# A gated MLP computed in rows, w_out's last rows on 16, 15 and 9 lanes, and an output of 360 and 280 columns with one store

## The chip, the cores and the metric

The kernel runs on one core of a Trainium2 chip. The metric is the device time of one execution in microseconds; for before it is the median of three runs. The engines are TensorE (PE, matmuls and transposes), VectorE (DVE), ScalarE (ACT), GpSimd (POOL) and SyncE (SP), which here only issues loads. 16 DMA engines move the data of all queues.

## The reference

One token of four sequences goes through a layer norm, then attention over a cache of 4096 positions in 32 heads of 128, and beside it a gated MLP; both are added to the token.

```python
xn = _layernorm(x, axis=-1)                       # x: 4 x 1 x 640, bf16
# attention
q = (xn @ wq).reshape(B, 1, 32, 128)              # wq: 640 x 4096
scores = einsum('bhqd,bhkd->bhqk', q, k_cache) * 128 ** -0.5   # caches: 4 x 32 x 4096 x 128
o = einsum('bhqk,bhkd->bhqd', softmax(scores), v_cache)
a = o.reshape(B, 1, 4096) @ wo                    # wo: 4096 x 640
# gated MLP
z = gelu(xn @ w_in)                               # w_in: 640 x 1728, tanh form
z1, z2 = z[..., :864], layernorm(z[..., 864:])
g = w_sp * z2 + b_sp                              # 1 x 1 and 1
m = (z1 * g) @ w_out                              # w_out: 864 x 640
out = x + a + m
```

The two caches are 268 MB of the 282 MB that are read.

## The kernel before

**Units.** The attention runs in 16 units: a unit is one batch and one group of 8 heads. Its keys and its values are 8.39 MB each. Each head takes 16 lanes, each lane 256 positions of 128 numbers, cut into four quarters (`NK = 4`).

**Places.** Keys go to `k_ring`, a ring of 7 quarters. Values go to `v_all`, which holds one unit. At the start `v_all` holds the weights: wq in its first 20,480 columns, w_in behind it, then the five full rows a lane of w_out. The rest of w_out lies in `p_m`, the place of the softmax's weights later on: one more row on 128 lanes, and 8 rows on each of 12 lanes, which are loaded in four loads of three lanes (`W_OUT`, `load_part`).

**The steps of a quarter n** (loop at L739): `product` (L537) multiplies the keys by the query on VectorE, `fold_half` (L543) adds halves on VectorE, `sums` (L555) adds the rest up on TensorE, and after every second quarter `row_sums` (L569) reads the result. At the end of a unit come the maximum, the exponentials (ScalarE), `by_head` (L607) and, a quarter later, `weighted` (L631), which multiplies by the values.

**The order of the loads** is a list (L195 to L203) that `pump` goes through: a load is written into the program as soon as the place it needs is marked free by the steps before it in the program. All of them are issued by SP, in this order, and each waits there for the semaphores of whatever it overwrites. There are eight semaphores for loads, given out in turn, so that a load also waits for an earlier one that used the same semaphore. The first entries are two quarters of unit 0's keys, `load_w` (w_in and the first parts of w_out), the other two quarters of unit 0, `load_w_few` (the part on few lanes), and unit 1's keys. `pump` runs for the first time at L237, ahead of the code for q. Unit 1's keys overwrite the quarter that unit 0's first step has used, so they wait for the first `sums`. Unit 0's values overwrite the weights in `v_all`, so they wait for the gated MLP. Unit 2's keys wait for the first `sums` of unit 1.

**q** (L297 to L314): 40 matmuls, chunk by chunk of wq (five rows a lane, 4096 columns each), into two PSUM tiles, which VectorE scales into `q_rows`. `stage_q` (L515) spreads the query of one unit over the lanes.

**The gated MLP** (`gmlp`, L397) is a generator whose pieces the loop calls in steps 0 and 1: z is made in columns (features on lanes), 140 small matmuls; gelu, the norm and the gate follow on VectorE and ScalarE; the products with w_out are 28 matmuls (L503) into `out_ps`, which x has entered already (L373).

**The output.** `out_ps` holds the 640 columns as two groups of 320, on lanes 0 to 3 and 32 to 35. At the end one copy (L823) takes both to SBUF, and two stores, on ScalarE's and SP's queues, write them.

Of the kernel before, what the change touches and what calls it, by code (L numbers as in the profile page):

```python
# [17 lines left out]
def kernel(  # L18
# [43 lines left out]
    W_OUT = ((P, 5, 1), (P, 1, 1), (12, 8, 4))  # L62
    assert sum(n * r for n, r, _ in W_OUT) == Fh
    NFC = sum(r for _, r, _ in W_OUT)

    def up(n):
        return -(-n // 256) * 256

    PW = sum(up(r * D) for _, r, _ in W_OUT[1:])
    NOH = D // 2  # L70
# [30 lines left out]
    nc.scalar.dma_start(out=x_bf, in_=A_x.flatten_outer_dims())  # L101
    v_all = places.tile([P, NK * QW], BF16, name="v_all")
# [6 lines left out]
    w_parts, f0, at_p = [], 0, 0  # L109
    for n, r, t in W_OUT:  # L110
        if f0 == 0:
            room = v_all[0:n, at_v : at_v + r * D]
        else:
            room = p_buf[0:n, at_p : at_p + r * D]
            at_p += up(r * D)
        w_parts.append((room.rearrange("p (k n) -> p k n", k=r), f0, n, r, t))
        f0 += n * r
    nc.sync.dma_start(out=wq_sb, in_=A_wq.rearrange("(p c) n -> p c n", c=DC))

    def load_part(part):  # L120
        w, f0, n, r, t = part
        rows = B_w_out[f0 : f0 + n * r].rearrange("(p k) n -> p k n", k=r)
        for l in range(t):
            nc.sync.dma_start(out=w[l:n:t], in_=rows[l:n:t])
# [12 lines left out]
    w_rows = [  # L137
        (w[:, i], f0 + i, n, r) for w, f0, n, r, _ in w_parts for i in range(r)
    ]
# [83 lines left out]
    def load_wo(hg):  # L223
        rows = A_wo[hg * HT * Dh : (hg + 1) * HT * Dh]
        if hg == HG - 1:
            by_head = rows.rearrange("(h p) n -> p h n", p=P)
            for h0, h1 in ((0, 2), (2, 4), (4, 6), (6, 7)):
                nc.sync.dma_start(out=wo_sb[:, h0:h1, :], in_=by_head[:, h0:h1, :])
            for half in range(2):
                cols = slice(half * NOH, (half + 1) * NOH)  # L230
                nc.sync.dma_start(out=wo_sb[:, HT - 1, cols], in_=by_head[:, HT - 1, cols])
            return
# [50 lines left out]
    wsp_bf = const.tile([1, 1], BF16)  # L283
    bsp_bf = const.tile([1, 1], BF16)
# [81 lines left out]
    out_ps = ps_out.tile([P, NOH], FP32)  # L366
    OG = 32

    def out_sum(half):
        return out_ps[OG * half : OG * half + Bsz, :]  # L370

    for half in range(2):
        nc.tensor.matmul(  # L373
            out=out_ps[OG * half : OG * half + OG, :],
            lhsT=ident[:Bsz, :OG],
            rhs=x_bf[:, half * NOH : (half + 1) * NOH],
            start=True,
            stop=False,
        )

    gm = {}
    for name in ("zz", "gw", "gt"):
        gm[name] = work.tile([P, 2, NFC, Bsz], FP32, name=name)
    gm["gz"] = work.tile([P, 3, NFC, Bsz], FP32, name="gz")
    nc.gpsimd.memset(gm["zz"][:], 0.0)
    gm["st"] = work.tile([1, 5 * Bsz], FP32, name="st")
    gm["ac"] = work.tile([1, 2 * Bsz], FP32, name="ac")
    gm["yT"] = work.tile([P, NFC, Bsz], BF16, name="yT")

    by_lanes = []  # L390
    for n, r, _ in W_OUT:
        if by_lanes and by_lanes[-1][0] == n:
            by_lanes[-1] = (n, by_lanes[-1][1] + r)
        else:
            by_lanes.append((n, r))

    def gmlp():  # L397
        zz, gw, gt, gz = (gm[n] for n in ("zz", "gw", "gt", "gz"))
        zT = ps_pv.tile([P, 2, NFC, Bsz], FP32, tag="pv", name="zT")
        for t in range(2):  # L400
            w_t = w_in_sb[:, :, t * Fh : (t + 1) * Fh]
            for k, (_, f, n, r) in enumerate(w_rows):
                for c in range(DC):
                    nc.tensor.matmul(
                        out=zT[0:n, t, k, :],
                        lhsT=w_t[:, c, f : f + (n - 1) * r + 1 : r],
                        rhs=xnT[:, c, 0:Bsz],
                        start=(c == 0),
                        stop=(c == DC - 1),
                    )  # L410
        yield
        k0 = 0
        for n, ks in by_lanes:
            nc.vector.tensor_copy(
                out=zz[0:n, :, k0 : k0 + ks, :], in_=zT[0:n, :, k0 : k0 + ks, :]
            )
            k0 += ks
        nc.vector.tensor_tensor(out=gw[:], in0=zz[:], in1=zz[:], op=ALU.mult)
        nc.vector.tensor_scalar(
            out=gw[:], in0=gw[:], scalar1=0.044715, scalar2=1.0, op0=ALU.mult, op1=ALU.add  # L420
        )
        nc.vector.tensor_tensor(out=gw[:], in0=gw[:], in1=zz[:], op=ALU.mult)
        nc.scalar.activation(
            out=gt[:], in_=gw[:], func=ACT.Tanh, scale=math.sqrt(2.0 / math.pi)
        )
        yield
        nc.vector.tensor_scalar(
            out=gt[:], in0=gt[:], scalar1=1.0, scalar2=0.5, op0=ALU.add, op1=ALU.mult
        )
        nc.vector.tensor_tensor(out=gz[:, 0:2], in0=zz[:], in1=gt[:], op=ALU.mult)  # L430
        sq = gz[:, 2, :, :]
        nc.vector.tensor_tensor(out=sq, in0=gz[:, 1, :, :], in1=gz[:, 1, :, :], op=ALU.mult)

        s_ps = ps_m.tile([1, 2, NFC, Bsz], FP32, tag="m", name="ln_ps")
        nc.tensor.matmul(
            out=s_ps[:], lhsT=ones_sq[:, 0:1], rhs=gz[:, 1:3], start=True, stop=True
        )
        yield
        st, ac = gm["st"], gm["ac"]
        mean_t = st[:, 0:Bsz]  # L440
        ex2_t = st[:, Bsz : 2 * Bsz]
        var_t = st[:, 2 * Bsz : 3 * Bsz]
        rst_t = st[:, 3 * Bsz : 4 * Bsz]
        tmp_t = st[:, 4 * Bsz : 5 * Bsz]
        nc.vector.tensor_reduce(
            out=st[:, 0 : 2 * Bsz].rearrange("o (s b) -> o s b", s=2),
            in_=s_ps[:].rearrange("o s k b -> o s b k"),
            axis=AX.X,
            op=ALU.add,
        )  # L450
        nc.vector.tensor_scalar(
            out=st[:, 0 : 2 * Bsz],
            in0=st[:, 0 : 2 * Bsz],
            scalar1=1.0 / float(Fh),
            scalar2=None,
            op0=ALU.mult,
        )
        nc.vector.tensor_tensor(out=tmp_t, in0=mean_t, in1=mean_t, op=ALU.mult)
        nc.vector.tensor_tensor(out=var_t, in0=ex2_t, in1=tmp_t, op=ALU.subtract)
        nc.scalar.activation(  # L460
            out=rst_t, in_=var_t, func=ACT.Sqrt, bias=eps_tile[:1], scale=1.0
        )
        wsp_t = work.tile([1, 1], FP32, name="wsp_t")
        nc.gpsimd.tensor_copy(out=wsp_t[:], in_=wsp_bf[:])
        bsp_t = work.tile([1, 1], FP32, name="bsp_t")
        nc.gpsimd.tensor_copy(out=bsp_t[:], in_=bsp_bf[:])
        yield
        nc.vector.reciprocal(out=rst_t, in_=rst_t)
        nc.vector.tensor_scalar(
            out=ac[:, 0:Bsz], in0=rst_t, scalar1=wsp_t[:, 0:1], scalar2=None, op0=ALU.mult  # L470
        )
        nc.vector.tensor_tensor(out=tmp_t, in0=ac[:, 0:Bsz], in1=mean_t, op=ALU.mult)
        nc.vector.tensor_scalar(
            out=ac[:, Bsz : 2 * Bsz],
            in0=tmp_t,
            scalar1=-1.0,
            scalar2=bsp_t[:, 0:1],
            op0=ALU.mult,
            op1=ALU.add,
        )  # L480
        ac_ps = ps_m.tile([P, 2 * Bsz], FP32, tag="m", name="ac_ps")
        nc.tensor.matmul(
            out=ac_ps[:], lhsT=ones_sq[0:1, :], rhs=ac[:], start=True, stop=True
        )
        ac_sb = work.tile([P, 2 * Bsz], FP32, name="ac_sb")
        nc.scalar.copy(out=ac_sb[:], in_=ac_ps[:])
        yield
        nc.vector.tensor_tensor(
            out=sq,
            in0=gz[:, 1, :, :],  # L490
            in1=ac_sb[:, None, 0:Bsz].to_broadcast([P, NFC, Bsz]),
            op=ALU.mult,
        )
        nc.vector.tensor_tensor(
            out=sq,
            in0=sq,
            in1=ac_sb[:, None, Bsz : 2 * Bsz].to_broadcast([P, NFC, Bsz]),
            op=ALU.add,
        )
        nc.vector.tensor_tensor(out=gm["yT"][:], in0=gz[:, 0, :, :], in1=sq, op=ALU.mult)  # L500
        for k, (w, _, n, _) in enumerate(w_rows):
            for half in range(2):
                nc.tensor.matmul(  # L503
                    out=out_sum(half),
# [351 lines left out]
```

## Time and profile before

| what | value |
|---|---|
| median of three runs (lowest, highest) | 662.18 us (661.91, 662.43) |
| the profiled execution | 662.09 us |
| its span, first to last instruction | 660.2 us |
| busy share: VectorE, TensorE, ScalarE, GpSimd | 79%, 48%, 5%, 2% |
| read from memory | 282.24 MB, 428 GB/s over the span |
| mean granted TensorE clock | 0.692 |
| wait of VectorE's `product` for keys | 87.9 us in 13 waits |

The page divides the span into 40 slices and prints for each engine the busy tenths (9 is 90% or more); for the DMA engines it is the mean share of the 16. In the timeline a line is: start us, length us, engine, source line, operation, tile written from tile read, count, and in brackets how long the engine had been idle and what it had waited for. `SPq` is SP's queue of issues. In the list of waits a line is: who waited, for whom, us in total, times, longest.

### The profile page before, as it was taken

To read this page: it belongs to the slowest core of one execution; us is meant where nothing else is said; L and a number is where in the kernel's file an instruction comes from. 1 tells how busy PE (TensorE), PEld (TensorE's weight loads), DVE (VectorE), ACT (ScalarE), POOL (GpSimd) and SP (SyncE) were. 2 spreads that over 40 slices of the span, in tenths; PEclk is the share of its full clock that TensorE was granted. 3 is DMA by queue.
4 is the path that set the end of the run, shared out by engine and by line. 5 is a ranking of instruction groups with operands and counts; after the bars stand their busy time and mean duration, and the time that the engine had idled before them with its cause. 6 is when DMAs were issued, how large, how long until landed. Compare 5 with 4: busy or idle time off the path is not lost.

```text
span 660.2 us, 4777 instructions
## 1 busy us (share of the span) xinstructions
PE 317.0 (48%) x2083; PEld 136.3 (21%) x2083; DVE 522.6 (79%) x276; ACT 29.9 (5%) x73; POOL 10.1 (2%) x20
## 2 busy tenths in 40 slices
PE   0574372526427363452636336263452534737367
PEld 0231121212213121120212112121120211212124
DVE  1767978959597795969959598695969969999950
ACT  0020000000000000000000000000000000000000
POOL 2300000000000000000000000000000000000000
PEclk9757676766767676585767768676685867676785
DMA  9999999999999999999999999999999999999997
GB/s 369 433 461 434 417 441 434 433 437 438 421 445 426 437 430 441 437 422 433 434 441 441 418 437 441 430 441 421 434 441 437 426 421 445 422 427 436 449 409 284
DMA packets 8232, 282.55 MB, mean 428 GB/s; under 512 B 892, under 2 KB 2184, under 8 KB 2568
## 3 DMA queue, kind: packets, MB, share of 16 engines
q1 hardware_dynamic: 8192, 282.25, 99.1%
q8 instruction: 16, 0.26, 0.1%
q10 hardware_dynamic: 20, 0.01, 0.0%
q14 instruction: 4, 0.03, 0.0%
HBM read 282.24 MB, written 0.01 MB: 428 GB/s over the span
## 4 chain that ended last, share of the span: by engine, by line
DMA 62%; DVE 28%; PE 8%; issue 1%; ACT 0%; DVEq 0%
DMA k_ring<-in_A_k_cache_dram 53%; DVE k_ring L537 14%; DVE k_ring L543 7%; PE s_ps L555 6%; DMA v_all<-in_A_v_cache_dram 4%; DMA k_ring<-in_A_wo_dram 3%; DVE s_sb L569 3%; DMA v_all<-in_A_wq_dram 2%; DVE p_m L607 1%; DVE m L578 1%; PE q_ps L303 1%; PE pv L631 1%; PE out_ps L699 1%; DVE p_m L678 1%; DVE mf L580 1%
## 5 line engine op out<-in xcount | busy, mean ns | idle before, releaser
L537 DVE TENSOR_TENSOR k_ring<-k_ring,qbc 128x8192 bf16<-128x8192 bf16 x64 | 282.9, 4420 | 88.5 <-DMA k_ring<-in_A_k_cache_dram 87.9
L555 PE MATMUL s_ps<-k_ring,ident 128*128 128x512 bf16 x512 | 202.2, 566 | 313.8 <-DVE k_ring L543 313.7
L555 PEld LDWEIGHTS <-ident 128*128 128x128 bf16 x512 | 64.0, 130 | 430.0 <-issue 245.4
L543 DVE TENSOR_TENSOR k_ring<-k_ring 128x4096 bf16<-128x4096 bf16 x64 | 145.9, 2280 | 1.1
L631 PE MATMUL pv<-v_all,p_m 128*32 128x512 bf16 x960 | 62.5, 419 | 0.0
L569 DVE TENSOR_REDUCE s_sb<-s_ps 128x128 f32<-128x1024 f32 x32 | 39.0, 1218 | 3.7 <-PE s_ps L555 3.7
L607 DVE TENSOR_TENSOR p_m<-p_c,own 128x2048 bf16<-128x2048 bf16 x16 | 36.6, 2285 | 0.7 <-ACT p_c L596 0.7
L631 PEld LDWEIGHTS <-p_m 128*32 128x32 bf16 x992 | 26.6, 106 | 42.5 <-issue 23.3
L596 ACT ACTIVATE p_c<-s_sb,nm 128x256 bf16<-128x256 f32 x16 | 8.1, 508 | 342.9 <-DVE nm L588 342.9
L662 PEld LDWEIGHTS o_ps<-o_rows,pick 128*128 128x128 f32 x96 | 20.4, 294 | 4.3 <-issue 3.3
L662 PE MATMUL o_ps<-o_rows,pick 128*128 128x128 f32 x96 | 19.1, 367 | 0.0
L643 ACT COPY o_rows<-pv 128x512 f32<-128x512 f32 x16 | 9.4, 586 | 165.7 <-PE pv L631 165.7
L311 DVE TENSOR_SCALAR q_rows<-q_ps 128x512 bf16<-128x512 f32 x2 | 1.4, 692 | 12.8 <-PE q_ps L303 12.8
L817 DVE TENSOR_TENSOR o_n_last<-o_last,rden_all 128x32 bf16<-128x32 f32 x1 | 0.2, 192 | 12.2 <-PE o_last L809 12.2
L303 PE MATMUL q_ps<-v_all,xnT 128*32 128x512 bf16 x40 | 4.5, 630 | 9.3 <-DMA v_all<-in_A_wq_dram 9.3
L527 ACT CAST qbc<-qbc_ps 128x128 bf16<-128x128 f32 x16 | 4.3, 266 | 97.6 <-PE qbc_ps L519 97.6
L578 DVE TENSOR_REDUCE m<-s_sb 128x1 f32<-128x256 f32 x16 | 6.7, 420 | 0.5
L519 PE MATMUL qbc_ps<-q_rows,of_row 128*128 128x128 bf16 x32 | 6.0, 276 | 0.6 <-DVE q_rows L311 0.6
L519 PEld LDWEIGHTS <-of_row 128*128 128x128 bf16 x32 | 4.1, 132 | 8.1 <-issue 7.4
L716 PE MATMUL o_last<-hot,o_rows 128*128 128x8 f32 x32 | 4.9, 279 | 0.7 <-ACT o_rows L643 0.7
L716 PEld LDWEIGHTS o_last<-hot,o_rows 128*128 128x128 f32 x32 | 4.8, 226 | 1.8 <-ACT o_rows L643 1.6
L699 PE MATMUL out_ps<-k_ring,p_m 128*4 128x320 bf16 x48 | 4.0, 309 | 2.1 <-DVE p_m L691 2.1
(87 smaller groups left out, 81.4 us busy)
## 6 DMA issues: line engine op xcount, KB each, us to landing
k_ring<-in_A_k_cache_dram SPq DMA_DIRECT2D x5, 4096.0 KB, 27.2
v_all<-in_A_v_cache_dram SPq DMA_DIRECT2D x2, 4096.0 KB, 28.2
v_all<-in_A_wq_dram SPq DMA_DIRECT2D x1, 5120.0 KB, 15.4
k_ring<-in_A_k_cache_dram SPq DMA_DIRECT2D x2, 2048.0 KB
k_ring<-in_A_v_cache_dram SPq DMA_DIRECT2D x1, 4096.0 KB
k_ring<-in_A_wo_dram SPq DMA_DIRECT2D x3, 1280.0 KB, 20.6
v_all<-in_B_w_in_dram SPq DMA_DIRECT2D x1, 2160.0 KB
k_ring<-in_A_v_cache_dram SPq DMA_DIRECT2D x1, 2048.0 KB
```

The source lines that it names most:

```text
L303: nc.tensor.matmul(out=q_ps[k * QD : (k + 1) * QD], lhsT=xnT[:, c, :], rhs=wq_v[:, c, k, e], start=(c == 0), stop=(c == DC - 1),)
L519: nc.tensor.matmul(out=qb_ps[:], lhsT=of_row[:, e, b].rearrange("p k f l -> p (k f l)"), rhs=q_rows[e][:, hg, :], start=(e == 0), stop=(e ...
L537: nc.vector.tensor_tensor(out=t, in0=t, in1=qbcs[u][:, None, :].to_broadcast([P, HC, Dh]), op=ALU.mult)
L543: nc.vector.tensor_tensor(out=t[:, :, 0:HD2], in0=t[:, :, 0:HD2], in1=t[:, :, HD2:Dh], op=ALU.add)
L555: nc.tensor.matmul(out=s, lhsT=ident[:], rhs=t[:, :, g * RW : (g + 1) * RW], start=(g == 0), stop=(g == m - 1),)
L569: nc.vector.tensor_reduce(out=scores[u][:].rearrange("p (r c) -> p r c", r=NK)[:, lo : hi + 1 : hi - lo], in_=sums_ps.pop(n // 2)[:], axis ...
L578: nc.vector.tensor_reduce(out=m1[:], in_=scores[u][:], axis=AX.X, op=ALU.max)
L607: nc.vector.tensor_tensor(out=p_m[:, u % 2], in0=p_c.pop(u)[:].rearrange("p (g c) -> p g c", c=CB)[:, :, :, None].to_broadcast([P, NG, CB, HT]
L631: nc.tensor.matmul(out=pvs[u][cg * QD : (cg + 1) * QD, :], lhsT=p_m[:, u % 2, g0 + n].rearrange("p c h -> p (c h)"), rhs=v_at[:, n * CB : ...
L662: nc.tensor.matmul(out=gr[hg][:], lhsT=pick[:, c, Bsz - 1 - b : P + Bsz - 1 - b], rhs=o[:, c, :], start=(b == 0 and c == 0), stop=(b == Bs ...
L699: nc.tensor.matmul(out=out_sum(half), lhsT=o, rhs=wo_sb[:, n, half * NOH : (half + 1) * NOH], start=False, stop=(hg == HG - 1 and n == HT ...
L716: nc.tensor.matmul(out=o_last[0][:, :, :, u % Bsz], lhsT=o[:, c, :], rhs=hot[:, c, :].rearrange("p (k e) -> p k e", e=PAR), start=(c == 0) ...
```

## The change

- `W_OUT` becomes four parts: five rows on 128 lanes in `v_all` as before, two rows on 16 lanes in `p_m`, and two parts of eight rows, on 15 and on 9 lanes, at the beginning of `v_all`. The last two use three of every four lanes and are loaded in three loads each; the 15 lanes belong to `load_w`, the 9 to `load_w_few`.
- The 1-element loads of w_sp and b_sp move from behind `stage_q(0)` to the beginning.
- `gmlp` makes z in rows: the four batches stay on lanes, the features lie along the row; four slices of 160 features share the array's column groups, the last 224 follow by themselves. Gelu, the norm and the gate work on rows of 384 numbers for each half. A transpose turns the gated rows into the columns that the products with w_out need, of which there are now 46.
- The scratch `gw` and the transposed `yT` lie in `v_all`, behind the two new parts.
- `out_ps` is cut at 360 columns, in all of x, w_out and wo; the end has two copies (VectorE and ScalarE) and one store.

```diff
-    W_OUT = ((P, 5, 1), (P, 1, 1), (12, 8, 4))
+    W_OUT = (
+        (P, 5, "v", 4, "first"),
+        (16, 2, "p", 4, "first"),
+        (15, 8, "q", 3, "first"),
+        (9, 8, "q", 3, "then"),
+    )
+    CUT = (0, 360, D)
+    places_w = {
+        "v": (v_all, up(DC * (HD + F))),
+        "p": (p_buf, 0),
+        "q": (v_all, 0),
+    }
+    for n, r, home, used, cuts in W_OUT:
+        t, at = places_w[home]
+        places_w[home] = (t, at + up(r * D))
+        lanes = n // used * GAP if used < GAP else n
+        room = t[0:lanes, at : at + r * D].rearrange("p (k n) -> p k n", k=r)
+        w_parts.append((room, f0, n, r, used, cuts))
+        f0 += n * r
+    at_g = places_w["q"][1]
+    def load_part(part, when):
+        w, f0, n, r, used, at = part
+        if at != when:
+            return
+        rows = B_w_out[f0 : f0 + n * r]
+        if used == GAP:
+            nc.sync.dma_start(out=w, in_=rows.rearrange("(p k) n -> p k n", k=r))
         else:
...
+            by_used = rows.rearrange("(q l k) n -> l q k n", l=used, k=r)
+            for l in range(used):
+                nc.sync.dma_start(out=w[l::GAP], in_=by_used[l])
     def load_w():
         nc.sync.dma_start(out=w_in_sb, in_=B_w_in.rearrange("(p c) n -> p c n", c=DC))
         for part in w_parts:
-            if part[4] == 1:
-                load_part(part)
+            load_part(part, "first")
     def load_w_few():
         for part in w_parts:
-            if part[4] > 1:
-                load_part(part)
+            load_part(part, "then")
...
+    zz = work.tile([P, 2, FW], FP32, name="zz")
+    gw = v_all[:, at_g : at_g + 4 * FW].bitcast(FP32).rearrange("p (t f) -> p t f", t=2)
+    at_g += up(4 * FW)
+    yT = v_all[:, at_g : at_g + NFC * QD].rearrange("p (k b) -> p k b", b=QD)
...
+        for c in range(DC):
+            for g in range(NQ):
+                nc.tensor.matmul(
+                    out=z_w[g * QD : (g + 1) * QD],
+                    lhsT=xnT[:, c, :],
+                    rhs=w_v[:, c, :, g * FN : (g + 1) * FN],
...
+        nc.scalar.mul(out=zz[:, :, 0:FN], in_=z_w[:], mul=0.5)
+        nc.scalar.mul(out=zz[0:QD, :, FN:FW], in_=z_r[0:QD], mul=0.5)
+        nc.vector.scalar_tensor_tensor(
+            out=gw, in0=zz[:], scalar=4 * 0.044715, in1=zz[:], op0=ALU.mult, op1=ALU.mult
+        )
...
+        for i, func in enumerate((ACT.Copy, ACT.Square)):
+            nc.scalar.activation(
+                out=gw[:, i], in_=zz[:, 1], func=func, accum_out=ss[:, i : i + 1]
+            )
...
+        nc.vector.transpose(
+            out=yT.rearrange("p k b -> p (k b)"), in_=yb[:].rearrange("p k b -> p (k b)")
+        )
+        k = 0
+        for w, _, _, r, _, _ in w_parts:
+            for i in range(r):
+                for half in range(2):
                     nc.tensor.matmul(
+                        out=out_sum(half),
+                        lhsT=yT[0 : w.shape[0], k, 0:Bsz],
+                        rhs=w[:, i, CUT[half] : CUT[half + 1]],
...
-        res = v_all[:, 0:NOH]
-        out_v = out.flatten_outer_dims()
-        nc.scalar.copy(out=res[0 : OG + Bsz], in_=out_ps[0 : OG + Bsz])
-        nc.scalar.dma_start(out=out_v[:, 0:NOH], in_=res[0:Bsz])
-        nc.sync.dma_start(out=out_v[:, NOH:D], in_=res[OG : OG + Bsz])
+        res = v_all[0:Bsz, 0:D]
+        nc.vector.tensor_copy(out=res[:, 0 : CUT[1]], in_=out_sum(0))
+        nc.scalar.copy(out=res[:, CUT[1] : D], in_=out_sum(1))
+        nc.scalar.dma_start(out=out.flatten_outer_dims(), in_=res)
```

The waits of the built program, as far as they concern the first loads and q (SP's queue in its order; a semaphore is one of the eight of the loads):

```
before  w_out 128x640 in p_m             waits x's semaphore
        keys of unit 0, second half      waits wq's
        w_out, 12 lanes, four loads      wait keys', keys' and the next two
        q, first matmul                  waits wq's
after   w_out 16 lanes in p_m            waits x's
        w_out 15 lanes, first load       waits wq's and w_in's
        w_out 15 lanes, two more         wait w_sp's, b_sp's
        keys of unit 0, second half      waits keys'
        w_out 9 lanes, three loads       wait keys', none, five full rows'
        q, matmuls of chunk 0            wait wq's or its follower's, and those of the two more
        q, matmuls of chunk 1            wait those of the three loads of 9 lanes
```

More of the change, by code (lines that the diff above doesn't have):

```diff
@@ L108 @@
     at_v = up(DC * (HD + F))
[L109 to L112, printed above, removed]
-        else:
[L114 to L124, printed above, removed]
+    w_parts, f0 = [], 0
+    places_w = {
[11 more added lines that the diff above has]
+    at_g = places_w["q"][1]
+    nc.sync.dma_start(out=wq_sb, in_=A_wq.rearrange("(p c) n -> p c n", c=DC))
+    def load_part(part, when):
[5 more added lines that the diff above has]
+            nc.sync.dma_start(out=w, in_=rows.rearrange("(p k) n -> p k n", k=r))
+        else:
+            by_used = rows.rearrange("(q l k) n -> l q k n", l=used, k=r)
+            for l in range(used):
+                nc.sync.dma_start(out=w[l::GAP], in_=by_used[l])
     def load_w():
@@ L229, in load_wo @@
             for half in range(2):
-                cols = slice(half * NOH, (half + 1) * NOH)
+                cols = slice(CUT[half], CUT[half + 1])
                 nc.sync.dma_start(out=wo_sb[:, HT - 1, cols], in_=by_head[:, HT - 1, cols])
@@ L364, with out_sum @@
     )
-    out_ps = ps_out.tile([P, NOH], FP32)
+    out_ps = ps_out.tile([P, max(CUT[1], D - CUT[1])], FP32)
     OG = 32
-    def out_sum(half):
-        return out_ps[OG * half : OG * half + Bsz, :]
+    def out_sum(half, rows=Bsz):
+        return out_ps[OG * half : OG * half + rows, 0 : CUT[half + 1] - CUT[half]]
     for half in range(2):
         nc.tensor.matmul(
-            out=out_ps[OG * half : OG * half + OG, :],
+            out=out_sum(half, OG),
             lhsT=ident[:Bsz, :OG],
-            rhs=x_bf[:, half * NOH : (half + 1) * NOH],
+            rhs=x_bf[:, CUT[half] : CUT[half + 1]],
             start=True,
@@ L379 @@
         )
[L381 to L395, printed above, removed]
@@ L397, in gmlp @@
-    def gmlp():
[L398 to L410, printed above, removed]
-        yield
[L412 to L420, printed above, removed]
-        )
-        nc.vector.tensor_tensor(out=gw[:], in0=gw[:], in1=zz[:], op=ALU.mult)
+    FW = FN + FR
@@ new lines @@
+    nc.gpsimd.tensor_scalar(
+        out=same[:],
+        in0=hot[:].rearrange("p c h -> p (c h)")[:, None, :].to_broadcast([P, NQ, QD]),
+        scalar1=1.0 / float(Fh),
+        scalar2=None,
+        op0=ALU.mult,
+    )
+    def gmlp():
+        w_v = w_in_sb.rearrange("p c (t f) -> p c t f", t=2)
+        z_w = ps_pv.tile([P, 2, FN], FP32, tag="pv", name="z_w")
+        for c in range(DC):
[4 more added lines that the diff above has]
+                    rhs=w_v[:, c, :, g * FN : (g + 1) * FN],
+                    start=(c == 0),
+                    stop=(c == DC - 1),
+                )
+        z_r = ps_pv.tile([P, 2, FR], FP32, tag="pv", name="z_r")
+        for c in range(DC):
+            nc.tensor.matmul(
+                out=z_r[0:QD],
+                lhsT=xnT[:, c, :],
+                rhs=w_v[:, c, :, NQ * FN : Fh],
+                start=(c == 0),
+                stop=(c == DC - 1),
+            )
+        yield
+        nc.scalar.mul(out=zz[:, :, 0:FN], in_=z_w[:], mul=0.5)
+        nc.scalar.mul(out=zz[0:QD, :, FN:FW], in_=z_r[0:QD], mul=0.5)
+        nc.vector.scalar_tensor_tensor(
+            out=gw, in0=zz[:], scalar=4 * 0.044715, in1=zz[:], op0=ALU.mult, op1=ALU.mult
+        )
+        nc.vector.scalar_tensor_tensor(
+            out=gw, in0=gw, scalar=1.0, in1=zz[:], op0=ALU.add, op1=ALU.mult
+        )
@@ L423, in gmlp @@
         nc.scalar.activation(
-            out=gt[:], in_=gw[:], func=ACT.Tanh, scale=math.sqrt(2.0 / math.pi)
+            out=gw, in_=gw, func=ACT.Tanh, scale=2 * math.sqrt(2.0 / math.pi)
         )
         yield
-        nc.vector.tensor_scalar(
-            out=gt[:], in0=gt[:], scalar1=1.0, scalar2=0.5, op0=ALU.add, op1=ALU.mult
-        )
-        nc.vector.tensor_tensor(out=gz[:, 0:2], in0=zz[:], in1=gt[:], op=ALU.mult)
-        sq = gz[:, 2, :, :]
-        nc.vector.tensor_tensor(out=sq, in0=gz[:, 1, :, :], in1=gz[:, 1, :, :], op=ALU.mult)
@@ L437, in gmlp @@
+        s_ps = ps_m.tile([P, 4], FP32, tag="m", name="ln_ps")
+        nc.tensor.matmul(
+            out=s_ps[:, 0:2],
+            lhsT=same[:].rearrange("p g m -> p (g m)"),
+            rhs=ss[:],
+            start=True,
+            stop=True,
+        )
+        nc.gpsimd.tensor_copy(out=wb[:, 0:1], in_=wsp_bf[:])
+        nc.gpsimd.tensor_copy(out=wb[:, 1:2], in_=bsp_bf[:])
+        nc.tensor.matmul(
+            out=s_ps[:, 2:4], lhsT=ones_sq[0:1, :], rhs=wb[:], start=True, stop=True
         )
@@ L438, in gmlp @@
         yield
[L439 to L449, printed above, removed]
+        nc.vector.tensor_copy(out=st[:, 0:4], in_=s_ps[:])
@@ new lines, in gmlp @@
+        nc.vector.scalar_tensor_tensor(
+            out=st[:, 4:5],
+            in0=st[:, 0:1],
+            scalar=st[:, 0:1],
+            in1=st[:, 1:2],
+            op0=ALU.mult,
+            op1=ALU.subtract,
+        )
+        nc.scalar.activation(
+            out=st[:, 5:6], in_=st[:, 4:5], func=ACT.Sqrt, bias=eps_tile[:], scale=-1.0
+        )
+        yield
+        nc.vector.reciprocal(out=st[:, 5:6], in_=st[:, 5:6])
+        nc.vector.tensor_tensor(
+            out=st[:, 6:7], in0=st[:, 5:6], in1=st[:, 2:3], op=ALU.mult
+        )
@@ L450, in gmlp @@
+        nc.vector.scalar_tensor_tensor(
+            out=st[:, 7:8],
+            in0=st[:, 0:1],
+            scalar=st[:, 6:7],
+            in1=st[:, 3:4],
+            op0=ALU.mult,
+            op1=ALU.subtract,
         )
         nc.vector.tensor_scalar(
[L452 to L455, printed above, removed]
+            out=zz[:, 1],
+            in0=zz[:, 1],
+            scalar1=st[:, 6:7],
+            scalar2=st[:, 7:8],
@@ L456, in gmlp @@
             op0=ALU.mult,
+            op1=ALU.subtract,
         )
[L458 to L461, printed above, removed]
-        )
-        wsp_t = work.tile([1, 1], FP32, name="wsp_t")
-        nc.gpsimd.tensor_copy(out=wsp_t[:], in_=wsp_bf[:])
-        bsp_t = work.tile([1, 1], FP32, name="bsp_t")
@@ L466, in gmlp @@
[L466 to L504, printed above, removed]
-                    lhsT=gm["yT"][0:n, k, :],
-                    rhs=w[:, half * NOH : (half + 1) * NOH],
-                    start=False,
-                    stop=False,
-                )
+        yield
@@ new lines, in gmlp @@
+        k0, f_at = 0, 0
+        for n, r, _, used, _ in W_OUT:
+            rows, fs = (P, FN) if k0 == 0 else (QD, n * r)
+            m = fs // r
+            u, v = (
+                zz[0:rows, t, f_at : f_at + fs].rearrange("p (q l i) -> p i q l", l=used, i=r)
+                for t in range(2)
+            )
+            to = yb[0:rows, k0 : k0 + r, 0 : m // used * GAP]
+            nc.vector.tensor_tensor(
+                out=to.rearrange("p i (q l) -> p i q l", l=GAP)[:, :, :, 0:used],
+                in0=u,
+                in1=v,
+                op=ALU.mult,
+            )
+            k0 += r
+            f_at += fs
@@ L701, in group_proj @@
                     lhsT=o,
[L702 removed]
+                    rhs=wo_sb[:, n, CUT[half] : CUT[half + 1]],
                     start=False,
```

39 lines of the change are left out of this document (25 added, 14 removed).

## The prediction

> **What bounds the kernel now.** First the page's slices of the span, then SyncE's own waits, the timeline of the first 90 us, its stretches by window, and the timeline of the end. The slices:
>
> ```profile
> DVE  1767978959597795969959598695969969999950
> DMA  9999999999999999999999999999999999999997
> GB/s 369 433 461 434 417 441 434 433 437 438 421 445 426 437 430 441 437 422 433 434 441 441 418 437 441 430 441 421 434 441 437 426 421 445 422 427 436 449 409 284
> ```
>
> The DMA engines are full from the first slice to the last, at about 434 GB/s; VectorE (DVE) is not. The time is 282 MB over that rate plus a start and an end. An edit costs time only if it leaves the DMA engines with nothing queued, or lengthens what follows the last load. The stretches of the start (core span, PE, PEld, DVE, ACT, POOL busy, clock, DMA share, GB/s):
>
> ```profile
> 0.00:30.00 30.00, 6.94 (x53) 2.77 (x54) 11.85 (x15) 1.84 (x3) 7.01 (x20) 0.91 0.94 394
> 30.00:35.00 5.00, 5.00 (x98) 3.79 (x97) 4.97 (x2) 1.55 (x2) 3.08 (x1) 0.84 1.11 470
> 35.00:45.00 10.00, 6.40 (x70) 3.23 (x70) 4.59 (x21) 3.08 (x5) 0.00 (x0) 0.50 1.06 456
> 45.00:75.00 30.00, 13.74 (x52) 4.71 (x49) 25.84 (x13) 0.85 (x3) 0.00 (x0) 0.61 1.00 431
> 75.00:85.00 10.00, 4.95 (x19) 1.53 (x21) 9.97 (x4) 0.27 (x1) 0.00 (x0) 0.67 0.99 427
> ```
>
> They add up to 11.82, 14.17, 18.73 and 31.66 MB moved by 30, 35, 45 and 75 us. What keeps the engines full is how early SyncE (SP) issues; from its waits and the timeline:
>
> ```profile
> SPq L164 <- DMA v_all<-in_B_w_in_dram: 2.1, 1, 2.1
> SPq L175 <- PE out_ps L503: 13.3, 1, 13.3
> ```
> ```profile
> 0.73 0.39 SPq L118 DMA_DIRECT2D v_all<-in_A_wq_dram  x1
> 16.12 0.33 SPq L164 DMA_DIRECT2D k_ring<-in_A_k_cache_dram  x1
> 16.15 4.46 PE L303 MATMUL q_ps<-v_all,xnT 128*32 128x512 bf16 x40 [9.30 <-DMA v_all<-in_A_wq_dram]
> 20.95 7.95 SPq L124 DMA_DIRECT2D p_m<-in_B_w_out_dram  x4
> 21.95 4.42 DVE L537 TENSOR_TENSOR k_ring<-k_ring,qbc 128x8192 bf16<-128x8192 bf16 x1 [0.60 <-ACT qbc L527]
> 32.04 0.34 SPq L164 DMA_DIRECT2D k_ring<-in_A_k_cache_dram  x1
> 46.29 0.33 SPq L175 DMA_DIRECT2D v_all<-in_A_v_cache_dram  x1
> 56.74 2.29 DVE L543 TENSOR_TENSOR k_ring<-k_ring 128x4096 bf16<-128x4096 bf16 x1
> 63.06 4.43 DVE L537 TENSOR_TENSOR k_ring<-k_ring,qbc 128x8192 bf16<-128x8192 bf16 x1 [4.03 <-DMA k_ring<-in_A_k_cache_dram]
> 75.45 0.33 SPq L164 DMA_DIRECT2D k_ring<-in_A_k_cache_dram  x1
> ```
>
> Sizes, from the shapes: wq 5.24 MB, each half of unit 0's keys 4.19, w_in 2.21, w_out 1.11 (0.82 in its five full rows), a unit's keys or values 8.39. Unit 1's keys are issued at 32.04, when 16.8 MB stand ahead of them and about 12.8 have been moved: the cover is some 9 us. The end is short:
>
> ```profile
> 657.43 0.42 ACT L823 CAST v_all<-out_ps 36x320 bf16<-36x320 f32 x1 [9.36 <-PE out_ps L699]
> 657.87 0.30 SPq L825 DMA_DIRECT2D out_dram<-v_all  x1
> ```
>
> **The change, part by part.**
>
> **1. The loads of w_out into wq's place.** Two new parts (15 and 9 lanes, eight rows each, three loads each) go to columns 0 to 10,240 of v_all, where wq lies, and their loads stand in the program before the q matmuls that read wq. The built program's list of waits shows what follows. The first load of the 15 lanes waits for wq and for w_in to land. The q matmuls of chunk 0 wait for the three loads of the 15 lanes, those of chunk 1 for the three of the 9 lanes too; in before they wait for wq alone. (The queries are then computed from a wq of which these lanes' first columns hold rows of w_out.) SP's queue is: wq, two quarters of unit 0's keys, w_in, w_out's 128 lanes, the 16 lanes, three loads of 15 lanes, the second half of unit 0's keys, three loads of 9 lanes, unit 1's keys.
>
> When w_in lands: SP's last small load starts at 28.2 us (L124's own rows, with 0.46 to 0.82 us each, median 0.65), ends at 28.9, and the wait above lasts 2.1: 31.0. So three loads at 0.65 run from 31.0 to 33.0, and unit 0's second half is issued at 33.0 instead of 16.12. From issue to flow I take 1.3 us: the first 5 us move 255 GB/s, 1.28 MB, which at 436 takes 2.9, so wq's flow began at 2.1, 1.35 after its issue. Flow from 34.3; the five full rows of w_out, the last ahead of it, land at 32.9 (issued at 3.40, 29.5 to landing). First gap: 1.4 us for the last engine, more for those done before.
>
> The half flows 4.19/0.436 = 9.6 us, to 43.9. The loads of 9 lanes are issued behind it (33.3 to 35.3) in the same queue. For a load behind others, the five full rows show the order: issued at 3.4, landed only when the 12.5 MB up to them had moved. No row of before gives a price for three rows of 10 KB behind a full queue: between 0.4 (one such row on an engine: 10,240 B at a sixteenth of 436) and 2.0 (three SP issues in a row); I take 1.2, three on one engine, as each load has three rows only. The q matmuls of chunk 1 start at 45.1.
>
> [...]
>
> From the first q matmul to unit 0's first product is 21.95 - 16.15 = 5.80 us; a fifth of the matmuls (0.9) is done during the wait: product at 50.0 instead of 21.95. Behind PE's wait stand qbc, the sums of unit 0 and z; for them wait VectorE, ScalarE and SP's load of unit 1's keys, which needs the first sums: 32.04 - 21.95 = 10.09 after the product, so issued at 60.1, flowing at 61.4. All else in the queue is done at 45.1. **Second gap: 17.5 us without keys or values to load**, against no cover.
>
> **2. The gated MLP in rows.** z: 20 matmuls of 320 columns, four at a time like q's (0.446 us for four of 512), 1.4 us, and 5 of 448, 1.9, instead of 4.6 for 140. That part ends as early as VectorE's fold. Then (before's 8.0 us from 36.68 to 44.70) by slopes of rows: three VectorE operations of 768 elements at 0.95 (0.15 us and 1.04 ns an element, from 4 and 112 elements at 0.15 and 0.27; it fits 1024 at 1.22), tanh 0.80, two ScalarE sums of 384 at 0.8, PE 0.4, sqrt with its table 1.3 of 1.28 + 0.30, four small ones 0.8, a scale of 384 at 0.5, four products 1.0, the transpose of 736 at 1.05 (256 took 0.46), and the two evictions after z 0.6 of which part lies behind the fold: 10.5 from 35.9, thus yT at 46.4 against 44.7, 1.7 later. Bounds 0 and 4. On before's path this is hidden by the 4.03 us for which VectorE waits at 63.06. Here VectorE is late and that cover is gone. The output matmuls are 46 at 0.15 (before's row: 10 in 1.50, 18 in 2.70), all now from v_all but four: unit 0's values are issued 6.9 after yT instead of 1.5: 50.0 + 24.34 + 1.7 + 5.4 = 81.4, flow 82.7. Unit 1's keys end at 61.4 + 19.2 = 80.6: 2.1 us gap.
>
> **3. Where VectorE is next late.** From product 0 to the end of unit 0's last fold is 59.03 - 21.95 = 37.1; with 1.7 that is 88.8, and unit 1's first product starts there (its keys have landed). Unit 2's keys are issued 75.45 - 63.06 = 12.4 later, at 101.2, flow at 102.5. The values end at 82.7 + 19.2 = 101.9: 0.6 us gap. Unit 2's keys land at about 121.8; VectorE needs some 32.5 us for unit 1 (38.7 from 63.06 to 101.78 less about 6.5 of idle, 87.9 over 13 waits) and is there at 121.3. From here the queue stays full.
>
> So unit 2's keys flow at 102.5. In before the 33.7 MB ahead of them have moved at 75 + (33.73 - 31.66)/0.427 = 79.8. **Loss at the start: 22.7 us** (it holds the gaps of 1.4, 17.5 plus part of the 9-lane loads, 2.1 and 0.6, and the unequal finish of the engines at the first one).
>
> **4. The end.** The two copies are not side by side: ScalarE's waits for VectorE in the built program. 360 columns on VectorE by q_rows' 512 at 0.69 are 0.53, 280 on ScalarE 0.38, with 0.05 between, against 0.42: +0.5. One store for two, side by side before: 0 (bounds -0.2, +0.3). Column groups of 360 and 280: a pair of output matmuls takes its longer half, 12% of the last group's 1.3 us of PE, +0.1, against a smaller last load, -0.1: 0.
>
> **5. At nothing:** the two 1-element loads go 21 us earlier on ScalarE's queue, beside wq; POOL's new memsets and `same` fall into its idle time after 5.5 us (it waits 21.5 us for one of those loads in before); 0.16 MB of 1,280-byte rows less, below 0.4 us by the mean rate, moved in other rows. If POOL were late, z's eviction would be; it has 50 us here.
>
> Sum: +22.7 + 0.5 = +23.2 on the profiled execution's 662.09 (span 660.2; 1.9 around it), whose runs have a median of 662.18: **685.3 us**. Bounds: 9-lane loads -0.8/+0.8, start of flow 1 to 2 us at three places -1/+2, the MLP's chain -1.7/+2.3, output matmuls hidden or not inside the 2.7 that VectorE sets anyway, gap of unequal engines -2/0. Together 680 to 690.
>
> **The rivals.**
> **A. VectorE's delay is kept.** Unit 1's first product is 25.7 us later than before (63.06 to 88.8). If the queue does not win back the 3 us between that and 22.7, as after a wait of other buffers, the time is 662.1 + 25.7 + 0.5 = 688.3. For it: VectorE's 79% leaves about 6 us a unit only. Against: those 6 us recur each unit.
> **B. The 9-lane loads don't stand behind the second half of the keys.** They land at about 37.7 (2.3 after issue at 35.3, as x from 0.73 to 3.01); all after it is 7.4 us earlier: 677.9. Against: the order seen above. [...]
> **C. Not slower.** The small loads land before wq is needed, because the wait on w_in is for something long done; q starts at 16.15, unit 1's keys are issued at 32, and the values, 7.1 later at 53.4, still precede the end of the keys at about 60. Only the end is left: 662.1 + 0.5 = 662.6. It decides if w_in's landing stood before 16 us. Against: 11.6 MB cannot move by then, only about 6 have.
> **D. The change does not do this:** the matmuls' waits turn out to be on the older loads of those queues; then q reads wq before it is overwritten or after, without delay, and the time is C's.
>
> **Chances.** Forecast 0.78, A 0.08, B 0.08, C and D together 0.06. The forecast's own range is 680 to 690; with A in it and B's upper part I give 677 to 690, leaving out C, D and the tails. 0.2% is 1.3 us, about what a measurement of this kernel can tell from no change: faster by more 0.02, within it 0.04, slower 0.94.
>
> **What will show it.** Right: q_ps idle until about 45 with a landing of w_out as its releaser, or in two pieces (about 35 and 45); product 0 near 50; unit 1's keys issued near 60; two slices of the page with a DMA digit well below 9 between 33 and 66 us and 9 after; the end 0.5 longer. Wrong: product 0 near 22 (C, D) or 42 (B); slices below 9 after 120 us (A, or an engine newly bound); a DMA rate lower throughout, which nothing above foresees.

## The result, and the profile after

The changed kernel takes 687.32 us (median of 5 runs, 687.1 to 689.6) against 661.91 for before in the same session: 3.9% slower, ratio 1.0392 with a 95% interval of 1.038 to 1.0404. The forecast was 685.3 in a range of 677 to 690. The profiled execution took 687.25 with a span of 685.3, that is 25.1 us more span than before.

The slices of the span, after:

```profile
DVE  1019899795969689596968969596996969999950
DMA  9864999999999999999999999999999999999996
GB/s 374 365 251 184 410 428 383 437 436 441 436 432 429 404 453 437 432 429 428 433 429 444 429 428 440 433 436 437 428 436 437 428 417 452 415 428 431 444 416 256
```

Slices two to four (17 to 69 us) are where before had 433, 461 and 434 GB/s. From the sixth slice on the DMA engines are as full as they were, but for the 383 GB/s of the seventh (103 to 120 us). So nearly all of the loss is in the first 70 us, and VectorE's row shows it on the other side: its second and third slices are nearly empty, where before computes. The timeline of the start (start us, length us, engine, line, operation, tiles, count, idle before and its releaser):

```profile
30.97 2.27 SPq L147 DMA_DIRECT2D v_all<-in_B_w_out_dram  x3
33.28 0.44 SPq L181 DMA_DIRECT2D k_ring<-in_A_k_cache_dram  x1
33.77 2.10 SPq L147 DMA_DIRECT2D v_all<-in_B_w_out_dram  x3
35.20 1.05 PE L318 MATMUL q_ps<-v_all,xnT 128*32 128x512 bf16 x8 [28.78 <-DMA v_all<-in_B_w_out_dram]
46.45 3.18 PE L318 MATMUL q_ps<-v_all,xnT 128*32 128x512 bf16 x32 [10.20 <-DMA v_all<-in_B_w_out_dram]
50.97 4.42 DVE L564 TENSOR_TENSOR k_ring<-k_ring,qbc 128x8192 bf16<-128x8192 bf16 x1 [0.60 <-ACT qbc L554]
61.37 0.34 SPq L181 DMA_DIRECT2D k_ring<-in_A_k_cache_dram  x1
79.40 0.33 SPq L192 DMA_DIRECT2D v_all<-in_A_v_cache_dram  x1
88.98 4.42 DVE L564 TENSOR_TENSOR k_ring<-k_ring,qbc 128x8192 bf16<-128x8192 bf16 x1
101.37 0.33 SPq L181 DMA_DIRECT2D k_ring<-in_A_k_cache_dram  x1
125.25 4.42 DVE L564 TENSOR_TENSOR k_ring<-k_ring,qbc 128x8192 bf16<-128x8192 bf16 x1 [4.37 <-DMA k_ring<-in_A_k_cache_dram]
```

The two PE lines show the cause: q's matmuls, which in before ran at 16.15 behind wq, now come in two pieces, and what ended each wait is a load of w_out, not of wq. Eight matmuls (chunk 0) are let go by the 15 lanes' loads, the other 32 by the 9 lanes' loads, 11 us later. Unit 1's keys go out at 61.37 instead of 32.04. The stretches between (us, busy of PE, PEld, DVE, ACT, POOL, clock, DMA share, GB/s):

```profile
30.00:35.00 5.00, 0.00 (x0) 0.00 (x0) 0.00 (x0) 0.00 (x0) 0.00 (x0) 1.00 0.70 242
35.00:40.00 5.00, 1.05 (x8) 0.17 (x8) 0.00 (x0) 0.00 (x0) 0.00 (x0) 1.00 0.89 380
40.00:45.00 5.00, 0.00 (x0) 0.00 (x0) 0.00 (x0) 0.00 (x0) 0.00 (x0) 1.00 0.88 380
45.00:50.00 5.00, 3.34 (x33) 1.34 (x34) 1.02 (x2) 0.00 (x0) 0.00 (x0) 1.00 0.03 12
50.00:55.00 5.00, 0.22 (x1) 0.10 (x1) 4.40 (x2) 0.27 (x1) 0.00 (x0) 0.75 0.00 0
55.00:60.00 5.00, 2.23 (x6) 0.85 (x6) 4.96 (x3) 0.00 (x0) 0.00 (x0) 0.50 0.00 0
60.00:65.00 5.00, 3.86 (x31) 1.62 (x29) 4.82 (x3) 1.78 (x4) 0.00 (x0) 0.73 0.61 210
...
100.00:105.00 5.00, 1.55 (x6) 0.56 (x5) 4.97 (x2) 0.27 (x1) 0.00 (x0) 0.50 0.78 275
```

Against 434 GB/s the stretch from 30 to 35 us lacks 2.2 us of data, 35 to 45 lacks 1.2, 45 to 60 nearly all of 15, 60 to 65 lacks 2.6; with 2.3 more between 100 and 110 us that makes some 23. The memory stands still for want of anything issued, while VectorE works.

The end, after, where before had one copy of 0.42:

```profile
682.24 0.52 DVE L847 CAST v_all<-out_ps 4x360 bf16<-4x360 f32 x1 [3.09 <-PE out_ps L726]
682.80 0.38 ACT L848 CAST v_all<-out_ps 4x280 bf16<-4x280 f32 x1 [10.00 <-DVE v_all L847]
683.21 0.27 ACTq L849 DMA_DIRECT2D out_dram<-v_all  x1
```

ScalarE's copy names VectorE's as its releaser: they run one after the other. From the start of the first copy to the store it takes 0.97 us instead of 0.44; from the store to the end of the span 2.09 instead of 2.33 (660.2 less 657.87).

### The profile page after: what moved, and what is told of

It reads as the page before. It is cut to its first block, busy times and chain, and to the rows that moved or that the text cites. A ratio compares the mean times of both kernels' runs of the same rounds, so it can differ in the third digit from the quotient of the medians.

```text
span 685.3 us, 4589 instructions
## 1 busy us (share of the span) xinstructions
PE 313.5 (46%) x1986; PEld 133.7 (20%) x1986; DVE 525.7 (77%) x272; ACT 32.1 (5%) x78; POOL 6.0 (1%) x22
## 4 chain that ended last, share of the span: by engine, by line
DMA 57%; DVE 32%; PE 8%; issue 1%; SPq 1%; ACT 1%; DVEq 0%
DMA k_ring<-in_A_k_cache_dram 46%; DVE k_ring L564 16%; DVE k_ring L570 7%; PE s_ps L582 6%; DMA k_ring<-in_A_wo_dram 5%; DMA v_all<-in_B_w_in_dram 4%; DVE s_sb L596 3%; DMA v_all<-in_B_w_out_dram 2%; DVE p_m L634 2%; DVE m L605 1%; PE out_ps L726 1%; DVE p_m L705 1%; DVE mf L607 1%; SPq L147 1%; PE q_ps L318 0%
## 5 line engine op out<-in xcount | busy, mean ns | idle before, releaser
L318 PEld LDWEIGHTS <-xnT 128*32 128x32 bf16 x40 | 1.4, 131 | 41.4 <-issue 30.3
L726 PE MATMUL out_ps<-k_ring,p_m 128*4 128x360 bf16 (+1 forms) x48 | 5.2, 357 | 1.8 <-DVE p_m L718 1.8
```

The lines of the kernel that those rows point to most:

```text
L726: nc.tensor.matmul(out=out_sum(half), lhsT=o, rhs=wo_sb[:, n, CUT[half] : CUT[half + 1]], start=False, stop=(hg == HG - 1 and n == HT - 1),)
```

## The experiments

Two factors were changed together, the form of the MLP and the place and order of w_out's last loads. The first four kernels separate them; the last four ask what is left once nothing waits.

**late15_9**: the new parts stay on wq's place, their loads are written into the program behind q's matmuls.

```diff
-        (15, 8, "q", 3, "first"),
-        (9, 8, "q", 3, "then"),
+        (15, 8, "q", 3, "late"),
+        (9, 8, "q", 3, "late"),
...
-            load_part(part, "then")
+            load_part(part, "late")
...
-    loads = [..., k_load(0, 2, 4), (load_w_few, []), k_load(1)]
+    loads = [..., k_load(0, 2, 4), (load_w_few, [Q_READ]), k_load(1)]
+    busy.remove(Q_READ)      # behind the code of q
+    pump()
```

> The changed kernel with the loads of both parts (15 and 9 lanes) put behind q's matmuls in the program; q reads wq unspoiled. Theory (the loss is q's wait for these loads): q starts at 16.2, unit 0's first product at 22, unit 1's keys are issued near 36. The built program's waits say that z's matmuls now wait for the six loads, which land behind the second half of unit 0's keys near 45, so the wait moves from q to z: z at about 45.4 instead of 32, yT near 58.7, unit 1's first product near 73 instead of 89, unit 2's keys issued near 85: 670.5 us (668 to 673). Rival 1 (the row form of the MLP costs the time, not q's wait): stays at 685 to 688. Rival 2 (nothing waits for small loads that matters): 662 to 663.

Measured: 669.85 us (668.96 to 670.93). In its timeline the wait stands where it was said to have gone, in front of z:

```profile
15.96 3.92 PE L319 MATMUL q_ps<-v_all,xnT 128*32 128x512 bf16 x40 [9.38 <-DMA v_all<-in_A_wq_dram]
45.84 1.52 PE L424 MATMUL z_w<-v_all,xnT 128*32 128x320 bf16 x20 [14.02 <-DMA v_all<-in_B_w_out_dram]
```
```profile
74.31 4.42 DVE L567 TENSOR_TENSOR k_ring<-k_ring,qbc 128x8192 bf16<-128x8192 bf16 x1
```

q is on time, z is 14 us late (45.84, in before 31.96), and unit 1's first product comes at 74.31 (63.06 in before). With the MLP in rows still there, 17.5 of the 25.4 us are gone.

**before_on_wq**: the MLP in columns, with the same kind of wait.

```diff
-        else:
+        elif t > 1:
+            room = v_all[0:n, 0 : r * D]
+        else:
             room = p_buf[0:n, at_p : at_p + r * D]
```

> The kernel before with one edit: the 12-lane part of w_out goes to wq's place, at columns 0 to 5,120 of v_all, in its four loads; the queries are then computed from a wq whose first columns on 12 lanes hold rows of w_out. The MLP stays in columns, the output stays as it was. Theory: q waits for all four loads; they are issued from 31.0 on (w_in's landing) and land behind the second half of unit 0's keys near 44.3; product 0 near 50, unit 1's keys issued near 60, unit 2's near 99.6, so 684.5 us (682 to 686.5). Rival 1 (the row form costs the time): 661.5 to 664.

Measured: 682.82 us (681.88 to 683.27), ratio to before 1.0314 (1.0299 to 1.033). All 40 matmuls wait for these loads, and the issue of unit 1's keys follows:

```profile
30.75 2.91 SPq L126 DMA_DIRECT2D v_all<-in_B_w_out_dram  x4
59.18 0.35 SPq L166 DMA_DIRECT2D k_ring<-in_A_k_cache_dram  x1
```
```profile
43.64 3.79 PE L305 MATMUL q_ps<-v_all,xnT 128*32 128x512 bf16 x40 [37.57 <-DMA v_all<-in_B_w_out_dram]
```

So 21 us of loss need no row form at all. With late15_9 this settles the cause of the greater part: it is the wait, not the new arithmetic. In this kernel the second half of unit 0's keys is issued at 3.97, not behind the loads into wq's place (33.28 in the changed kernel), and q starts 2.8 us earlier than there; the 4.5 us between the two kernels were not taken apart further.

**nine_ahead** and **nine_after_q** move the three loads of 9 lanes alone, ahead of the second half of unit 0's keys, or behind q.

```diff
 nine_ahead
-    loads = [..., (load_w, []), k_load(0, 2, 4), (load_w_few, []), k_load(1)]
+    loads = [..., (load_w, []), (load_w_few, []), k_load(0, 2, 4), k_load(1)]
 nine_after_q
-    loads = [..., (load_w, []), k_load(0, 2, 4), (load_w_few, []), k_load(1)]
+    loads = [..., (load_w, []), k_load(0, 2, 4), (load_w_few, [Q_READ]), k_load(1)]
+    busy.remove(Q_READ)      # behind the code of q
+    pump()
```

> The changed kernel with the three loads of 9 lanes put ahead of the second half of unit 0's keys in SP's queue; the queries are computed from the same overwritten wq. Theory (these loads are late because 4.19 MB stand ahead of them in the same queue): they land near 37.3, product 0 at about 41.8 instead of 51.0, unit 1's keys issued near 52.2, unit 2's near 92.2: 677.9 us (676 to 680). Rival B of the prediction turned round (the loads are late for a reason of their own, few lanes or their issue): 685 to 688.

Measured: 677.76 us (676.59 to 679.4).

> The changed kernel with only the three loads of 9 lanes put behind q's matmuls in the program; q is computed from a wq with the 15 lanes' columns overwritten. Theory: q waits for the 15 lanes alone, starts at 35.2 and runs through, product 0 at about 40.8, unit 1's keys issued near 51.2, unit 2's near 91.2: 676.9 us (675 to 679). Rival (the 15 lanes' loads set q's end as well, or the gap in the queue at 33 us is the larger loss): 682 to 688.

Measured: 675.8 us (674.78 to 676.2). From nine_ahead, then from nine_after_q:

```profile
35.05 1.04 PE L318 MATMUL q_ps<-v_all,xnT 128*32 128x512 bf16 x8 [28.16 <-DMA v_all<-in_B_w_out_dram]
37.83 3.61 PE L318 MATMUL q_ps<-v_all,xnT 128*32 128x512 bf16 x32 [1.74 <-DMA v_all<-in_B_w_out_dram]
```
```profile
35.20 4.46 PE L319 MATMUL q_ps<-v_all,xnT 128*32 128x512 bf16 x40 [28.73 <-DMA v_all<-in_B_w_out_dram]
```

Put ahead of 4.19 MB, the same three loads land 8.6 us sooner (37.83 against 46.45) and the time falls by 9.6. They were late because of what stood in front of them in the queue. The 15 lanes alone, as the second fence shows, hold q until 35.20 whatever follows.

**rows_full_lanes** and **rows_old_end** take q's and z's new waits away: w_out's last 224 rows as 16 and 12 full lanes, one load each, behind q.

```diff
-        (16, 2, "p", 4, "first"),
-        (15, 8, "q", 3, "first"),
-        (9, 8, "q", 3, "then"),
+        (16, 8, "q", 4, "then"),
+        (12, 8, "q", 4, "then"),
+    # load_w_few waits for Q_READ, as in nine_after_q
 rows_old_end, besides
-    CUT = (0, 360, D)
+    CUT = (0, D // 2, D)
+    # one copy on ScalarE and two stores, as in before
```

> The changed kernel with w_out's last rows as two parts of 16 and 12 lanes (every lane used, one load each, 42 output matmuls instead of 46), in wq's place, loaded behind q's matmuls in the program. MLP in rows, 360 and 280 columns, two copies and one store all kept. Theory: nothing of the start waits, product 0 near 22, unit 1's keys issued near 32; yT near 45.7, about 1 us later than before, inside the 4 us for which VectorE waits before unit 1's first product; only the end is left, +0.5 for the copies one after the other and about -0.25 for the single store: 662.2 us (661.7 to 662.8). Rival (the row form costs by itself): 664 or more.

Measured: 665.2 us (664.75 to 665.73), ratio 1.0049 (1.0036 to 1.0062): the expectation failed by 3 us.

> The same kernel with the end of before: two groups of 320 columns, one copy on ScalarE, two stores. Theory: 0.25 us less than with two copies and one store, so 661.9 us (661.5 to 662.4), not to be told from before. Rival (the groups of 360 and 280 with one store save time): 0.3 us more than with them or worse.

Measured: 664.86 us (664.58 to 664.95). This expectation failed by 3 us too. The medians of the two ends differ by 0.34 us where 0.25 was said, but their runs overlap; the 3 us are in both. They could have been the row form. But in the trace of rows_full_lanes product 0 starts at 21.45, unit 1's keys go out at 31.85, and VectorE is ready for unit 1 earlier than the keys are, so its chain is hidden as forecast. What is late is the landing. Unit 1's first product (63.06 after 4.03 us of waiting in before):

```profile
65.24 4.42 DVE L566 TENSOR_TENSOR k_ring<-k_ring,qbc 128x8192 bf16<-128x8192 bf16 x1 [5.77 <-DMA k_ring<-in_A_k_cache_dram]
```

Stretches of before, then of rows_full_lanes:

```profile
40.00:48.00 8.00, 6.99 (x34) 2.74 (x34) 5.16 (x11) 1.75 (x3) 0.00 (x0) 0.50 1.08 466
48.00:56.00 8.00, 4.12 (x14) 1.31 (x11) 8.00 (x4) 0.00 (x0) 0.00 (x0) 0.53 0.97 420
```
```profile
40.00:48.00 8.00, 7.37 (x40) 3.79 (x42) 6.07 (x11) 2.89 (x4) 0.00 (x0) 0.57 1.11 337
48.00:56.00 8.00, 4.58 (x26) 1.74 (x23) 8.00 (x4) 0.00 (x0) 0.00 (x0) 0.65 0.91 393
```

The DMA engines are as busy as in before (share 1.11) and move a quarter less: packets take longer. In the trace's packet records before's 12 rows of 10,240 B take 0.38 us each; the 28 rows here take 0.92 on average and up to 1.54, from 40.9 to 44.8 us. A stretch of the view counts a packet where it starts; with each packet's bytes spread over its own time, the records give 292 GB/s from 40 to 48 us, against 433 in before. The packets of 64 KB of unit 1's keys that start between 41 and 46 us take 2.6 to 4.9 us each, 2.42 in before, so what stands behind the rows is slow too. That gave a new theory, that rows for neighbouring lanes get in each other's way, and two more kernels, both with the end of before, the last rows as 32 lanes of seven rows in `p_m`, and one difference between them.

```diff
+        (32, 7, "p", 4, "then"),
 rows_32_four, besides, in load_part
-            nc.sync.dma_start(out=w, in_=rows.rearrange("(p k) n -> p k n", k=r))
+            by_lane = rows.rearrange("(p k) n -> p k n", k=r)
+            step = 1 if n == P else 4
+            for l in range(step):
+                nc.sync.dma_start(out=w[l:n:step], in_=by_lane[l:n:step])
```

> MLP in rows with the end of before, w_out's last 224 rows as one part of 32 lanes with seven rows each (8,960 B a lane, 24 output matmuls), in p_m, one load behind the second half of unit 0's keys; nothing of w_out lies on wq. Theory (the 3 us left in the two kernels with 16 and 12 lanes are the DMA engines held up by rows that go to neighbouring lanes: 28 rows of 10 KB took 0.92 us each instead of 0.38, and the rate fell from 434 to 176 GB/s for 2 us): twice the lanes spread the same bytes twice as wide, so about a quarter of that loss, 0.7 us, is left: 662.6 us (662.0 to 663.3). Rival (the 3 us belong to the row form: its chain, its ScalarE and VectorE work, its 42 matmuls): 664.3 or more.

Measured: 663.26 us (662.97 to 663.55).

> The same kernel with the 32 lanes loaded in four loads of every fourth lane, as before did with its 12 lanes. Theory: neighbouring lanes are no longer written at once, rows take 0.34 us each (8,960 B against 10,240 at 0.38), no rate dip at 42 us: 661.9 us (661.5 to 662.3), the time of before, with the MLP in rows. Rival: as in the run beside it, 664.3 or more; a second one, that the order of lanes does not matter, only their number: the same as the run beside it.

Measured: 662.77 us (662.55 to 662.93), ratio to before 1.0011 (1.0003 to 1.002); that is above the range expected, while rows_32_one lies inside its own. The rows of 8,960 B take 0.44 us on average and up to 0.66 in one load, 0.34 every time in four. From rows_32_one, then rows_32_four:

```profile
40.00:48.00 8.00, 6.87 (x36) 3.01 (x36) 6.01 (x10) 2.96 (x5) 0.00 (x0) 0.64 1.15 448
48.00:56.00 8.00, 3.43 (x8) 1.16 (x9) 8.00 (x4) 0.00 (x0) 0.00 (x0) 0.57 0.94 410
```
```profile
40.00:48.00 8.00, 6.13 (x36) 2.90 (x36) 5.00 (x10) 3.97 (x7) 0.00 (x0) 0.69 1.08 464
48.00:56.00 8.00, 2.41 (x6) 0.88 (x7) 8.00 (x4) 0.00 (x0) 0.00 (x0) 0.53 1.00 434
```

466, 337, 448 and 464 GB/s in the same 8 us go with 0.38, 0.92, 0.44 and 0.34 us a row; with packets spread over their time, 433, 292, 386 and 431. The dip comes from how the rows are loaded: same bytes, same lanes, same row form in the last two, and four loads of every fourth lane have none. Whether it is that neighbouring lanes are written at once, or that 32 rows instead of eight stand in one load, these two kernels do not separate; eight neighbouring lanes a load were not built. Unit 2's first product lags before by 2.34 us in rows_full_lanes, 0.92 in rows_32_one and -0.29 in rows_32_four, so the row form of the MLP costs nothing at the start. By the packet records these kernels moved 2.6, 0.9 and 0.1 us' worth of data less than before between 40 and 50 us, which is about the lag. Each time was above its forecast, though: rows_32_four is 0.84 above before, and its profile shows where that execution lost it:

```profile
656.00 2.05 PE L727 MATMUL out_ps<-k_ring,o_n_last 128*4 128x320 bf16 x12 [1.28 <-DMA k_ring<-in_A_wo_dram]
```

At the very end PE waits 1.28 us for wo, which it does not in before. Why wo lands later there, with the values landing earlier (653.14 against 653.60), was not settled. No version here beats before.

## Why the prediction was right

- **The mechanism** stands: q's wait for loads that overwrite wq, behind w_in and then behind 4.19 MB, is shown by the releasers in the timeline, made in a kernel without the row form (before_on_wq, 20.9 us), and shortened as worked out in three others (17.5, 9.6 and 11.5 us less; 16.8, 9.4 and 10.4 had been expected, against the measured 687.3).
- **The first gap**: 15 lanes issued at 30.97 (31.0 forecast), the half of the keys at 33.28 (33.0).
- **The 9 lanes' loads**: chunk 1 at 46.45, forecast 45.1. The half of the keys had been given 9.6 us at full rate; the stretches from 35 to 45 show 380 GB/s. By the packet records it took from 34.4 to 45.6. That some engines had the 15 lanes' rows before it is likely, but was not tested. The term of 1.2 us, three rows on one engine, was an estimate that no row of before shows. It came out: the nine rows run in three chains of three, one behind the other, 0.38 to 0.44 us a row, from 44.7 to 46.0. They only began at 44.7 instead of 43.9, and q started 0.5 after the last of them.
- **From issue to flow**: 1.3 us had been taken. The first packet of unit 1's keys, on an empty queue, starts at 62.34, 1.0 after the issue, the lower of the bounds.
- **From q to unit 1's keys**: product 0 at 50.97 (50.0) and the keys at 61.37 (60.1), the delay of the step before carried on. The second gap is the 45 to 62 us of the stretches.
- **The MLP in rows**: unit 0's values at 79.40, 28.4 after product 0 where 31.4 had been forecast. The output matmuls took 4.6 us instead of 6.9; their price came from a stretch at a granted clock of 0.50, and here the stretch from 75 to 80 us has 0.84; that the clock made the difference was not tested. The chain up to yT was 0.6 shorter too.
- **VectorE next late**: unit 1's first product at 88.98 (88.8), unit 2's keys issued at 101.37 (101.2). The gap before the values, 2.1, did not come; about as much, 2.3, was lost at 100 to 110 us. VectorE set the sum either way, as the bounds had it. VectorE was ready for unit 2 at 120.9 (121.3), but the keys were there at 125.25 where 121.8 had been worked out. The same working gives 99.0 for before, where the product started at 101.78. So it has a load of keys landing some 3 us too early on both sides, and the difference of the two sums, the forecast, hides that.
- **The start's loss**: 22.7 forecast; unit 2's first product is 23.5 later than before (125.25 against 101.78).
- **The end**: +0.5 forecast; +0.53 for the copies and -0.24 for the store.
- **What is missing from 23.2 to the 25.1 of the span**: 0.8 at the start, and 1.2 at the end. The lag goes from 23.43 to 24.71 between the first products of units 4 and 5, where the first load of wo falls, but it is back at 23.53 by unit 13 and stands there at unit 15. At the last values it is 24.73 again. Where those last 1.2 us come from stays open. Rival A, that VectorE's delay of 25.7 is kept, forecast 688.3, nearer to 687.32 than the 685.3, but not this course: the delay was 25.92 at unit 1 and fell to 23.47 at unit 2, where VectorE waits for keys again. The time alone would not have told the two apart.
- **Rivals B, C and D** fell with the timeline: the 9 lanes did stand behind the keys, and q did wait.

## What to carry to other kernels

Where a place is used twice, the order of the program decided here who waits: with the loads written ahead of the last reader of what they overwrite, q's matmuls ran at 35.20 and 46.45 us, with the loads behind it at 15.96 (late15_9). This kernel, bound by its loads, lost about the time for which nothing was issued (25.1 us of span, of which the stretches show some 23), so look for the one load whose issue hangs on the delayed step (unit 1's keys, 61.37 instead of 32.04), and compare the delay with the bytes still queued ahead of it. Rows for a few neighbouring lanes did better here in loads of every fourth lane (662.77 against 663.26 us).

## What the runs showed of the hardware that was not expected

28 rows of 10 KB on lanes 0 to 15 and 0 to 11, one load each, held all the engines' rate at 337 GB/s over 8 us, where before has 466, and made the kernel about 2.3 us later at unit 2; a tenth of a per cent of the bytes did that. With 32 lanes in one load the rate was 448 GB/s and unit 2 0.92 us later than before; in four loads of every fourth lane it was 464, and unit 2 was not later (-0.29). Against rows_32_four, which has no dip, the lags are 2.63 and 1.21.

The lengths of single rows say more. The shortest row of 10,240 B took 0.38 us, of 8,960 B 0.34. The longest took 1.54 with 16 and 12 neighbouring lanes, four times as much, and 0.66 with 32, about twice. In rows_32_four, in loads of every fourth lane, every row took 0.34. But the changed kernel's 15 lanes, also in loads of every fourth lane, took 0.39 to 0.70 us a row of 10,240 B, from 32.6 to 34.8 us. Why rows took longer, no run shows.
